# Banded attention and a gated product on one core: w_out decoded in pairs, more small buffers, and a new written order

## The chip, the core and the metric

The kernel runs on one core of a Trainium2 chip: TensorE for matrix products (PE in the profile, PEld its weight loads), VectorE (DVE), ScalarE (ACT), GpSimd (POOL) and SyncE (SP), which issues most DMAs; ScalarE issues the rest. All inputs lie in HBM, the result goes back there. The metric is the time of one execution on the device, in microseconds (us).

## The reference, cut to what matters

```python
# attention: batch 8, heads 8, 512 local and 32 global positions, head size 64
k_all, v_all = concat(k_g, k_l), concat(v_g, v_l)
out_g = sm(scale * q_g @ k_all.T) @ v_all            # global queries see all keys
s_ll = where(abs(i - j) <= 32, scale * q_l @ k_l.T, -1e9)
out_l = sm(concat(scale * q_l @ k_g.T, s_ll)) @ concat(v_g, v_l)
x = heads_joined(concat(out_g, out_l))               # [8, 544, 512]
# gated product
gate = sigmoid(sum(conv_w[k] * x shifted by k - 4 for k in range(5)))
out = (gate * (x @ w_val)) @ w_out                   # [8, 544, 512]
```

The weights w_val, conv_w and w_out arrive as 64-bit floats (their type in the reference is kept as it comes), and the kernel decodes them from pairs of 32-bit words on the chip.

## The kernel before, in words

A *unit* u (32 of them) is one batch with one pair of heads; batch b has units 4b to 4b+3. For each unit: `s` (score products into two PSUM banks, 64 small matmuls), `mx` (VectorE: mask, negated scale and row maximum, L490; for five early units the mask is added by TensorE and L486 takes the maximum), `exp` (ScalarE, L503), `den` and `rec` (VectorE), `norm` (scaling by the reciprocal, one half of a unit at a time, on VectorE L521 or as four ScalarE instructions L519), `t` (VectorE transposes, L528). Two units together give one product with the values, `av`. `xc` copies its result from PSUM, `halo` sets the four columns ahead of it, `xh` and `xl` split it into two parts that TensorE multiplies at its faster rate, `tap` and `conv` are the five taps of the convolution on VectorE (for four units TensorE does them with diagonal weights: `dg`, `pc`), and `sig` is the sigmoid.

The global queries go by batch: `gs` (scores), `gmax` and `gng` (maximum, negated), `gexp`, `gt` (transposes on TensorE), `gtc` (copy), `gav`, `gden`, `grec`, `gnorm`, `gx`, `gxc`.

The gated product goes by batch too: `g1.b.e.t` (three matmuls of 512 columns, L628, in which block t of x meets block e of w_val), `gv` (times the gate), `gh`, `gl` (the two parts again), `g2.b.r.e` (three matmuls, L665), `ob` (copy out of PSUM), `st` (store). A last, smaller pass with the key g does the global rows of all batches.

**The order** is a text, `ORDER`: a list of some 2,000 task names, which the program runs through once. Each engine gets its instructions in this order and keeps to it. A name's `:ACT`, `:DVE` or `:SP` says which engine does a task that several could do; `@36` says which of the eight PSUM banks it takes (`gs0@36`: banks 3, 4 and 6, 7). A task that writes a bank waits for all that still reads it. `z17.1` is 17 matmuls of zeros into bank 1: they fill TensorE's time at the start. A planner made the list; it is not in the program.

Loads go out on SP's queue in the list's order, and each one also waits until TensorE has done the last matmul that stands ahead of it in the list (`transfer`). A load whose buffer is still read holds up all that is behind it in the queue.

The weights are decoded in eight steps `s0` to `s7` (`f64_parts`) and a rounding `high`. The four column blocks of w_val are decoded in two pairs, with buffers that later hold gh and gl. The four row blocks of w_out are decoded singly, and take their raw words from a buffer of the attention's `pm` rotation and the working copy from the output's `ob` rotation.

Of the kernel before, what the change touches and what calls it, by code (L numbers as in the profile page):

```python
# [82 lines left out]
cw dg0:DVE s0@30 dg1:DVE dg2:ACT mx0.0 mx0.1 ng0 s1@52 dg3:DVE exp0.0 mx1.0 mx1.1 z6.0@1 gs0@36 exp0.1 ng1 s2@01  # L83
exp1.0 den0 rec0 norm0.1:DVE norm0.0:DVE t0 exp1.1 den1 w0.s0:ACT gmax0.0 rec1 norm1.0:ACT mx2.0 norm1.1:ACT gmax0.1
mx2.1 gng0 gexp0.0 w0.s1 ng2 exp2.0 exp2.1 t1 z17.1@5 av0@42 w0.s2 w0.s3 w0.s4 wi4 w0.high:ACT den2 w0.s5 w2.s0:ACT
gexp0.1 rec2 w0.s6 w2.s1 iq4 iq5 xc0:ACT z8.2@0 s3@07 w0.s7 norm2.1:ACT gt0.0@4 w2.s2 mx3.0 halo0 gt0.1@5 mx3.1
norm2.0:ACT t2 pc0.0@1 ng3 w4.s0:ACT ig3 xh0:ACT gtc0.0 gtc0.1 xc1:ACT w4.s1 ig2 w2.s3 exp3.0 exp3.1 w4.s2 xl0
w2.high:ACT w4.s3 pc0.1 pc0.2 wi5 pc0.3 w2.s4 w4.high:ACT ig0 ig1 s4@23 w4.s4 halo1 den3 iq6 iq7 w4.s5 rec3
norm3.0:ACT w4.s6 s5@05 pc0.4 norm3.1:DVE w5.s0:ACT mx4.0 mx4.1 xh1:ACT conv0.3:ACT pc1.0@7 w4.s7 ng4 w5.s1 pc1.1
pc1.2 exp4.0 t3 w5.s2 gav0@6 gden0 ig6 mx5.0 exp4.1 exp5.0 mx5.1 exp5.1 grec0 pc1.3 pc1.4 w5.s3 av1@20 w2.s5 gnorm0  # L90
gx0@6 den4 w5.s4 xc3:ACT gxc0:ACT xl1 conv1.3:ACT w5.high:DVE g1.0.1.0@5 ig5 xc2:ACT rec4 den5 w2.s6 w5.s5 iv2
halo2:DVE g1.0.1.1 gs1@60 halo3:DVE iq8 w5.s6 rec5 w5.s7 w2.s7 s6@23 mx6.0 gmax1.0 mx6.1 norm4.1:ACT gmax1.1
norm4.0:ACT xh2:DVE norm5.1:ACT pc2.0@4 pc2.1 exp6.0 gng1 pc2.2 pc2.3 iq9 ig4 fix0 exp6.1 pc2.4 pc3.0@3 den6 gexp1.0
xl2 gexp1.1 t4 pc3.1 gt1.0@6 gt1.1@0 ig7 xh3:DVE norm5.0:ACT pc3.2 conv2.3:ACT gtc1.0 iv3 fix1 s7@47 gtc1.1 rec6
norm6.0:ACT t5 mx7.0 wi6 s8@10 iq10 mx7.1 norm6.1:ACT g1.0.3.0@6 g1.0.0.0@4 t6 xl3 exp7.1 exp7.0 pc3.3 mx8.0 mx8.1
pc3.4 gav1@7 exp8.0 conv3.3:ACT w6.s0:DVE gden1 den7 w6.s1 g1.0.1.2 grec1 rec7 exp8.1 g1.0.0.1 sig0 w6.s2 norm7.1:DVE
# [89 lines left out]
FIRST = "q0 q1 w0 q2 q3 w1 v0 w2 w3 v1 m0"  # L186
NX = 10
XC = 3
NH = 9
NHF = 2  # L190
NV = 2
NPC = sum(f"pc{u}.0" in BY for u in range(NU))
# [6 lines left out]
def attention_moe(ctx, tc, qk, vw, vgw, maskd, fard, w_val, convT, w_out, out):  # L199
# [103 lines left out]
    def weight(k):  # L303
# [31 lines left out]
        for m in range(8):  # L335
            tasks[f"w{k}.s{m}"] = lambda m=m: step(m)
# [530 lines left out]
```

## Time and profile before

| | us |
|---|---|
| median of three runs | 344.08 (343.84 to 345.83) |
| the profiled execution | 342.64 |
| its span from first to last instruction | 340.9 |
| TensorE, busy in the span | 330.6 (97%) |
| VectorE | 319.5 (94%) |
| ScalarE | 285.0 (84%) |
| mean DMA rate | 178 GB/s, 60.67 MB in all |

The span is what the profile's times count from; the execution's own time is 1.7 us longer. Busy time is the union of an engine's instructions. Waits, branches and DMA issues are not in it. Ends of matmuls are modelled, so TensorE can be slower than its best pace and still show as busy.

### The profile page before, as it was taken

The numbers are of one execution on the slowest core, as the hardware profiler recorded it, in microseconds if no ns is written. First come the engines' busy times: TensorE is split into PE (matmuls) and PEld (weight loads), VectorE is DVE, ScalarE is ACT, GpSimd is POOL, SyncE is SP. The second block draws the span as 40 slices with busy tenths as digits, with TensorE's granted clock in tenths as the row PEclk, the third lists the DMA queues.
The fourth block names the chain that finished last, engine by engine and source line by source line (L and its number), as shares of the span: only waits on it lengthen the run. The fifth ranks groups of instructions, "written<-read, shape, count | busy, mean of one in ns | idle before, by whom it ended". The sixth has DMA issues, their size and how long they took to land.

```text
span 340.9 us, 15502 instructions
## 1 busy us (share of the span) xinstructions
PE 330.6 (97%) x6575; PEld 254.8 (75%) x6575; DVE 319.5 (94%) x987; ACT 285.0 (84%) x926; POOL 0.8 (0%) x7
## 2 busy tenths in 40 slices
PE   7899999999999999999999999999999999999995
PEld 4475566768877867788778687788787787888894
DVE  6899999999999999999899999999999998998981
ACT  3899999989999999999999899999998869314240
POOL 0000000000000000000000000000000000000000
PEclk9999999999999999999999999999999999999999
DMA  7969868726672358577845471596322712002032
GB/s 276 385 206 322 313 210 257 280 68 237 240 236 80 105 173 336 162 232 262 294 105 184 167 271 45 198 336 181 135 72 74 253 15 95 4 31 92 2 123 63
DMA packets 20037, 60.67 MB, mean 178 GB/s; under 512 B 2304, under 2 KB 4736, under 8 KB 19968
## 3 DMA queue, kind: packets, MB, share of 16 engines
q1 hardware_dynamic: 18528, 57.01, 48.8%
q10 hardware_dynamic: 1440, 2.67, 2.2%
q8 instruction: 51, 0.84, 1.0%
q14 instruction: 18, 0.15, 0.1%
HBM read 50.76 MB, written 8.91 MB: 175 GB/s over the span
## 4 chain that ended last, share of the span: by engine, by line
PE 83%; DMA 6%; ACT 5%; DVE 3%; issue 1%; ACTq 0%; SPq 0%; DVEq 0%
PE psum L628 28%; PE psum L665 25%; PE psum L542 10%; PE psum L469 8%; PE psum L606 4%; PE psum L422 3%; DMA wraw<-in_w_val_dram 3%; PE psum L404 2%; PE psum L381 2%; DMA vg<-in_vgw_dram 2%; ACT pm L519 1%; DMA qk<-in_qk_dram 1%; ACT pm L503 1%; ACT xc L284 1%; PE psum L439 1%
## 5 line engine op out<-in xcount | busy, mean ns | idle before, releaser
L503 ACT ACTIVATE pm<-pm,mx 128x128 f32<-128x128 f32 x216 | 83.9, 395 | 0.8 <-DVE mx L490 0.7
L588 DVE SCALAR_TENSOR_TENSOR gate<-xc,cw,gate 128x512 f32<-128x512 f32 x112 | 80.6, 744 | 0.8 <-ACT gate L278 0.3
L665 PE MATMUL psum<-woh,gh 128*128 128x512 f32 x128 | 52.2, 408 | 0.7 <-ACT pg L396 0.5
L628 PE MATMUL psum<-xh,wvh 128*128 128x512 f32 x128 | 52.7, 412 | 0.0
L628 PE MATMUL psum<-xh,wvl 128*128 128x512 f32 x128 | 50.6, 395 | 0.0
L628 PE MATMUL psum<-xl,wvh 128*128 128x512 f32 x128 | 50.5, 395 | 0.0
L519 ACT ACTIVATE pm<-pm,mx 128x128 f32<-128x128 f32 x160 | 50.5, 400 | 0.0
L665 PE MATMUL psum<-woh,gl 128*128 128x512 f32 x128 | 50.1, 391 | 0.0
L665 PE MATMUL psum<-wol,gh 128*128 128x512 f32 x128 | 50.1, 391 | 0.0
L490 DVE CUSTOM_DVE_ANT_0 pm<-psum,mask 128x128 f32<-128x128 f32 x216 | 48.4, 286 | 1.4 <-PE psum L469 1.3
L542 PEld LDWEIGHTS psum<-pts,v 32*64 32x64 f32 x2560 | 35.9, 130 | 8.2 <-issue 2.5
L503 ACT ACTIVATION_READ_ACCUMULATOR pm<-pm,mx 128x1 f32 x216 | 41.8, 194 | 0.0
L528 DVE STREAM_TRANSPOSE pts<-pm 128x1024 f32<-128x1024 f32 x32 | 39.4, 1235 | 0.5 <-ACT pm L519 0.3
L542 PE MATMUL psum<-pts,v 32*64 32x96 f32 (+3 forms) x2560 | 38.9, 259 | 0.8 <-ACT pg L396 0.6
L469 PE MATMUL psum<-qk 64*32 64x128 f32 x2048 | 36.3, 272 | 0.9 <-issue 0.5
L469 PEld LDWEIGHTS psum<-qk 64*32 64x32 f32 x2048 | 29.5, 105 | 7.5 <-issue 4.2
L665 PEld LDWEIGHTS psum<-woh,gh 128*128 128x128 f32 x128 | 24.1, 188 | 7.8 <-issue 1.4
L284 ACT COPY ob<-psum 128x512 f32<-128x512 f32 x30 | 17.4, 579 | 14.8 <-PE psum L665 13.6
L628 PEld LDWEIGHTS psum<-xh,wvh 128*128 128x128 f32 x128 | 24.3, 190 | 7.2 <-issue 1.0
L628 PEld LDWEIGHTS psum<-xh,wvl 128*128 128x128 f32 x128 | 24.0, 188 | 5.7
L665 PEld LDWEIGHTS psum<-woh,gl 128*128 128x128 f32 x128 | 24.0, 188 | 5.4
L628 PEld LDWEIGHTS psum<-xl,wvh 128*128 128x128 f32 x128 | 24.1, 188 | 4.6
(120 smaller groups left out, 542.1 us busy)
## 6 DMA issues: line engine op xcount, KB each, us to landing
qk<-in_qk_dram SPq DMA_DIRECT2D x30, 768.0 KB, 6.0
vg<-in_vgw_dram SPq DMA_DIRECT2D x32, 325.0 KB, 3.7
v<-in_vw_dram SPq DMA_DIRECT2D x16, 640.0 KB, 5.5
out_dram<-ob SPq DMA_DIRECT2D x26, 256.0 KB, 3.9
wraw<-in_w_val_dram SPq DMA_DIRECT2D x4, 512.0 KB, 11.1
wraw<-in_w_out_dram SPq DMA_DIRECT2D x4, 512.0 KB, 4.0
out_dram<-ob ACTq DMA_DIRECT2D x6, 256.0 KB, 2.0
qk<-in_qk_dram ACTq DMA_DIRECT2D x1, 480.0 KB, 3.8
```

The source lines that it names most:

```text
L284: A.copy(out, in_)
L422: on_pe(T.matmul(ag[SG * c:SG * c + SG, :], pgt[:, R * h + a if a < R else 2 * R, SG * c:SG * c + SG], vt[:, a, h, :], start=(a == 0), sto ...
L469: on_pe(T.matmul(s[h][C * j:C * j + C, i, :], qkt[rows, C * QAT[m]:C * QAT[m] + C], blocks(qkt[rows], b, (C * ahead, 2), (C * near, 2), (1 ...
L490: V.tensor_tensor_reduce(out=pm[:, h, i, :], in0=s[:, i, :], in1=mask[:, (c0 + i > 0) + (c0 + i == HB - 1), :], op0=ALU.add, op1=ALU.min, ...
L503: A.activation(out=pm[:, h, i, :], in_=st[u]["s"][h][:, i, :] if ON_PE[u] else pm[:, h, i, :], func=AF.Exp, bias=mx[:, c:c + 1], scale=SCA ...
L519: A.activation(out=p[:, i, :], in_=p[:, i, :], func=AF.Copy, scale=rec[:, i:i + 1])
L528: V.transpose(out=st[w, "pts"][:, :, R * k:R * k + R].rearrange("p h i a q -> p h (i a q)"), in_=st[u]["pm"].rearrange("p h i c -> p h (i ...
L542: on_pe(T.matmul(x[j // 2][D * h:D * h + D, j % 2, C * first:C * (first + count)], vt[rows, slot, h, :], p, start=(slot == 0), stop=stop))
L588: V.scalar_tensor_tensor(out=acc, in0=xc[:, k:k + SL], scalar=cw[:, u % NDT, k:k + 1], in1=acc, op0=ALU.mult, op1=ALU.add)
L606: on_pe(T.matmul(bank(f"pc{u}.0"), diag[n][:, c, :], st[u]["xc"][:, k:k + SL], start=(k == 0), stop=(k == KW - 1)))
L628: on_pe(T.matmul(bank(f"g1.{key}.{e}.0")[:, :n], w[:, e, t * P:t * P + P], x, start=(t == 0 and q == 0), stop=(t == NDT - 1 and q == 2)))
L665: on_pe(T.matmul(bank(f"g2.{key}.{r}.0"), g, w, start=(e == 0 and q == 0), stop=(e == NDT - 1 and q == 2)))
```

## The change

Three things change in the code, and the whole list of the order.

w_out is decoded in pairs like w_val: 1024 columns at a time, in 2 x 8 steps instead of 4 x 8. Its raw words get a buffer of their own (`wr`, one, for two pairs one after the other), the working copy too (`wa`). The statistics `mx` have six buffers instead of three, and each could hold two units; since the list still names `den` for every unit, every unit gets its own and den and rec stay as they were. Two buffer counts (`NPM`, `NPT`) keep their values under a name. The DMA scratch of the compiler is set to 1024.

The list is another one throughout. By its tags, on the whole: three halves of norm go from VectorE to ScalarE (40 to 43 on ScalarE), three xh casts (21 to 24), two ob copies (30 to 32) and the one gxc copy; four gh casts go from ScalarE to VectorE (11 to 15 there) and three xc copies (0 to 3). taps and halos keep their numbers, 14 loads of ScalarE's function tables stay 14. The zero matmuls at the start are 6, 12 and 13 instead of 6, 17 and 8.

```diff
 ORDER = """
-cw dg0:DVE s0@30 dg1:DVE dg2:ACT mx0.0 mx0.1 ng0 s1@52 dg3:DVE exp0.0 mx1.0 mx1.1 z6.0@1 gs0@36 exp0.1 ng1 s2@01
...
+cw dg0:DVE dg1:DVE s0@46 mx0.0 mx0.1 ng0 s1@10 dg2:DVE exp0.0 exp0.1 mx1.0 mx1.1 ng1 den0 exp1.0 rec0 norm0.0:DVE
...
@@ -187,6 +186,9 @@
 NX = 10
 XC = 3
 NH = 9
+NMX = 6
+NPM = 3
+NPT = 2
 NHF = 2
 NV = 2
 NPC = sum(f"pc{u}.0" in BY for u in range(NU))
@@ -267,7 +269,7 @@
 
     def taps():
         raw = craw.rearrange("p (n two) -> p n two", two=2)
-        a = rotating([P, NDT * KW], I32, tag="mx", name="cva", bufs=3)
+        a = rotating([P, NDT * KW], I32, tag="mx", name="cva", bufs=NMX)
         for step in f64_parts(raw, a, None):
             step()
         V.tensor_tensor(out=cw.rearrange("p t k -> p (t k)"), in0=a.bitcast(F32), in1=raw[..., 0].bitcast(F32),
@@ -303,19 +305,15 @@
     def weight(k):
         of_val = k < NDT
         c = k % NDT
-        n = 2 if of_val else 1
         src = w_val if of_val else w_out
         whi, wlo = (wvh, wvl) if of_val else (woh, wol)
         box = {}
 
         def load():
-            if of_val:
-                if c % 2 == 0:
-                    wraws["pair", c] = rotating([P, 2, 2 * DM], I32, tag=("gh", "gl")[c // 2], name=f"wraw{k}", bufs=1)
-                raw = wraws["pair", c // 2 * 2][:, c % 2]
-            else:
-                raw = box["raw"] = rotating([P, 1, 2 * DM], I32, tag="pm", name=f"wraw{k}", bufs=3)
-                raw = raw[:, 0]
+            if k % 2 == 0:
+                wraws["pair", k] = rotating([P, 2, 2 * DM], I32, tag=("gh", "gl")[c // 2] if of_val else "wr",
+                                           name=f"wraw{k}", bufs=1)
+            raw = wraws["pair", k // 2 * 2][:, k % 2]
             if of_val:
                 transfer(raw.rearrange("p (t n) -> p t n", t=NDT),
                          src[:, c * P:c * P + P].bitcast(I32).rearrange("(t p) n -> p t n", p=P))
@@ -324,17 +322,18 @@
 
         def step(m):
             if m == 0:
-                raw = wraws["pair", c] if of_val else box["raw"]
-                raw = raw.rearrange("p w (n two) -> p w n two", two=2)
-                box["a"] = rotating([P, n, DM], I32, tag="pts" if of_val else "ob", name=f"wa{k}", bufs=2)
-                box["steps"] = f64_parts(raw, box["a"], wlo[:, c:c + n, :], lambda m: BY[f"w{k}.s{m}"])
+                raw = wraws["pair", k].rearrange("p w (n two) -> p w n two", two=2)
+                tag, bufs = ("pts", NPT) if of_val else ("wa", 1)
+                box["a"] = rotating([P, 2, DM], I32, tag=tag, name=f"wa{k}", bufs=bufs)
+                box["steps"] = f64_parts(raw, box["a"], wlo[:, c:c + 2, :], lambda m: BY[f"w{k}.s{m}"])
             box["steps"][m]()
 
         wraws[k] = load
         tasks[f"wi{k}"] = load
-        for m in range(8):
-            tasks[f"w{k}.s{m}"] = lambda m=m: step(m)
-        tasks[f"w{k}.high"] = lambda: copy(f"w{k}.high", whi[:, c:c + n, :], box["a"].bitcast(F32))
+        if k % 2 == 0:
+            for m in range(8):
+                tasks[f"w{k}.s{m}"] = lambda m=m: step(m)
+            tasks[f"w{k}.high"] = lambda: copy(f"w{k}.high", whi[:, c:c + 2, :], box["a"].bitcast(F32))
 
     loads, values = {}, {}
 
@@ -472,13 +471,17 @@
         st[u] = {"s": s}
 
     def open_p(u):
-        st[u]["pm"] = rotating([P, 2, R, P], F32, tag="pm", name=f"pm{u}", bufs=3)
+        st[u]["pm"] = rotating([P, 2, R, P], F32, tag="pm", name=f"pm{u}", bufs=NPM)
 
     def l_max(u, h):
         s = st[u]["s"][h]
         c0 = R * (u % 2)
         if h == 0:
-            st[u]["mx"] = rotating([P, 16], F32, tag="mx", name=f"mx{u}", bufs=3)
+            if u % 2 == 0 or f"den{u}" in BY:
+                both = rotating([P, 2, 16], F32, tag="mx", name=f"mx{u}", bufs=NMX)
+            else:
+                both = st[u - 1]["both"]
+            st[u]["both"], st[u]["mx"] = both, both[:, u % 2 if f"den{u // 2 * 2 + 1}" not in BY else 0]
             if not ON_PE[u]:
                 open_p(u)
         pm, mx = st[u].get("pm"), st[u]["mx"]
@@ -504,12 +507,15 @@
                          bias=mx[:, c:c + 1], scale=SCALE if ON_PE[u] else -1.0,
                          accum_out=mx[:, 8 + c:9 + c])
 
+    def sums(u):
+        return st[u]["mx"][:, 8:16] if f"den{u // 2 * 2 + 1}" in BY else st[u]["both"][:, :, 8:16]
+
     def l_den(u):
-        den = st[u]["mx"][:, 8:16]
+        den = sums(u)
         V.tensor_scalar(out=den, in0=den, scalar1=1e-9, scalar2=None, op0=ALU.add)
 
     def l_rec(u):
-        den = st[u]["mx"][:, 8:16]
+        den = sums(u)
         V.reciprocal(den, den)
 
     def l_norm(u, h):
@@ -523,7 +529,7 @@
     def l_turn(u, h):
         w, k = divmod(u, 2)
         if (w, "pts") not in st:
-            st[w, "pts"] = rotating([P, 2, HB, R, C], F32, tag="pts", name=f"pts{w}")
+            st[w, "pts"] = rotating([P, 2, HB, R, C], F32, tag="pts", name=f"pts{w}", bufs=NPT)
         if h is None:
             V.transpose(out=st[w, "pts"][:, :, R * k:R * k + R].rearrange("p h i a q -> p h (i a q)"),
                         in_=st[u]["pm"].rearrange("p h i c -> p h (i c)"))
@@ -850,7 +856,7 @@
     from concourse.bass_utils import run_bass_kernel_spmd as _run
 
     laid = _layout(_np, **inputs)
-    nc = _bacc.Bacc("TRN2", target_bir_lowering=False, num_devices=1)
+    nc = _bacc.Bacc("TRN2", target_bir_lowering=False, num_devices=1, dynamic_dma_scratch_size=1024)
     arrays, args = {}, []
     for name in _INS:
         a = _np.ascontiguousarray(laid[name])
```

Three places in the instruction order follow. Names there are tiles: gm is the maximum of the global scores, mx and pm the statistics and exponentials of a unit, wraw a weight's raw words, wa its working copy.

VectorE in batch 2, where the global scores' maximum is taken. Before:

```order
L259 SCALAR_TENSOR_TENSOR wol<-wraw_1090 128x512
L389 TENSOR_REDUCE gm_1413<-psum 128x1 x2
L490 ISA pm_1421,mx_1420<-psum,mask 128x128
L490 ISA mx_1420 128x1
L490 ISA pm_1421,mx_1420<-psum,mask 128x128
L490 ISA mx_1420 128x1
L490 ISA pm_1421,mx_1420<-psum,mask 128x128
L490 ISA mx_1420 128x1
L490 ISA pm_1421,mx_1420<-psum,mask 128x128
L490 ISA mx_1420 128x1
L393 TENSOR_SCALAR gm_1413<-gm_1413 128x2
L642 TENSOR_TENSOR gl_1334<-gv_0_1335,gh_1333 128x512
```

and now:

```order
L260 TENSOR_SCALAR wraw_1006<-wa_1127 128x1024
L288 CAST gh_1303<-gv_0_1305 128x512
L642 TENSOR_TENSOR gv_1_1371<-psum,gate_952 128x512
L388 TENSOR_REDUCE gm_1374<-psum 128x1
L288 CAST gh_1303<-gv_1_1371 128x512
L388 TENSOR_REDUCE gm_1374<-psum 128x1
L648 TENSOR_TENSOR gl_1304<-gv_1_1371,gh_1303 128x512
L392 TENSOR_SCALAR gm_1374<-gm_1374 128x2
L493 ISA pm_1400,mx_1399<-psum,mask 128x128
L493 ISA mx_1399 128x1
```

Before, the negation (L393) stands behind four mask steps and their reads of the accumulator; now (L392) it stands ahead of all of them, and the two maxima have other work between them.

ScalarE near the start, from the first decode step of the second w_val pair to the copies of the transposed global block (pgt). Before:

```order
L248 ACTIVATE wa_477<-wraw_99 128x1024
L396 ACTIVATE pg<-psum,gm_343 128x544
L284 COPY xc_487<-psum 128x512
L519 ACTIVATE pm_362<-pm_362,mx_350 128x128 x8
L248 ACTIVATE wa_568<-wraw_472 128x512
L284 CAST xh_572<-xc_487 128x512
L410 COPY pgt_575<-psum 128x512
L410 COPY pgt_575<-psum 128x640
L284 COPY xc_578<-psum 128x512
L503 ACTIVATE pm_584,mx_551<-psum,mx_551 128x128 x8
```

and now:

```order
L250 ACTIVATE wa_499<-wraw_99 128x1024
L286 COPY xc_506<-psum 128x512
L286 CAST xh_555<-xc_506 128x512
L409 COPY pgt_563<-psum 128x512
L280 ACTIVATE diag_235<-ident,cw 128x128
L280 ACTIVATE diag_570<-ident,cw 128x128 x4
L525 ACTIVATE pm_476<-pm_476,mx_370 128x128 x4
L409 COPY pgt_563<-psum 128x640
L286 CAST wvh<-wa_499 128x1024
L506 ACTIVATE pm_587,mx_576<-psum,mx_576 128x128 x8
L506 ACTIVATE pm_675,mx_674<-pm_675,mx_674 128x128 x4
```

The second pgt copy (128x640) stood right behind the first; now five diagonal pieces and a scaling of four stand between the two, and the second xc copy with its xh cast ahead of both.

SyncE's queue around the last loads of w_out. Before:

```order
L296 DMA v_1039<-in_vw_dram 128x1280
L296 DMA wraw_1090<-in_w_out_dram 128x1024
L296 DMA qk_1124<-in_qk_dram 128x1536
L296 DMA qk_1230<-in_qk_dram 128x1536
L296 DMA vg_1237<-in_vgw_dram 128x650
L296 DMA wraw_1342<-in_w_out_dram 128x1024
L296 DMA vg_1533<-in_vgw_dram 128x650
```

and now:

```order
L298 DMA vg_974<-in_vgw_dram 128x650
L298 DMA wraw_1006<-in_w_out_dram 128x1024 x2
L298 DMA v_1084<-in_vw_dram 128x1280
L298 DMA qk_1099<-in_qk_dram 128x1536
L298 DMA qk_1180<-in_qk_dram 128x1536
L298 DMA v_1294<-in_vw_dram 128x1280
```

Before, the four blocks of w_out were loaded at four places of the queue; now there are two, two loads each, and the second, which needs the buffer of the first, has the v load of the third pair of units right behind it.

## Rows read from the trace of the kernel before

**Rows 1.** busy time of each engine over the span, from the page.

```profile
PE 330.6 (97%) x6575; PEld 254.8 (75%) x6575; DVE 319.5 (94%) x987; ACT 285.0 (84%) x926; POOL 0.8 (0%) x7
```

**Rows 2.** stages: us, then busy PE, PEld, DVE, ACT, POOL, granted clock, DMA.

```profile
30.00:165.00 135.00, 133.67 (x3096) 99.33 (x3096) 132.36 (x478) 132.76 (x456) 0.00 (x0) 1.00 0.63 217
165.00:205.00 40.00, 39.02 (x794) 30.66 (x793) 38.04 (x132) 37.29 (x121) 0.00 (x0) 1.00 0.58 193
205.00:290.00 85.00, 84.68 (x1851) 67.38 (x1850) 82.58 (x236) 76.98 (x240) 0.00 (x0) 1.00 0.43 141
290.00:335.00 45.00, 45.00 (x298) 38.01 (x281) 39.88 (x80) 14.02 (x30) 0.00 (x0) 1.00 0.13 48
```

**Rows 3.** timeline at 205 us: start, duration, engine, line, operation, tiles.

```profile
205.37 0.40 PE L628 MATMUL psum<-xh,wvh 128*128 128x512 f32 x1
205.04 0.29 DVE L490 CUSTOM_DVE_ANT_0 pm<-psum,mask 128x128 f32<-128x128 f32 x1
205.25 0.29 DVE L490 CUSTOM_DVE_ANT_0 pm<-psum,mask 128x128 f32<-128x128 f32 x1
205.47 0.69 DVE L584 TENSOR_TENSOR xl<-xc,xh 128x512 fp32r<-128x512 f32 x1
```

**Rows 4.** groups by shape: operation, tiles, count, busy us, mean ns, idle before.

```profile
L256 DVE SCALAR_TENSOR_TENSOR wa<-wraw,wa 128x512 int32<-128x512 int32 x4 | 2.7, 678 | 0.0
L256 DVE SCALAR_TENSOR_TENSOR wa<-wraw,wa 128x1024 int32<-128x1024 int32 x2 | 2.4, 1217 | 0.0
L263 DVE TENSOR_SCALAR wraw<-wraw 128x512 int32<-128x512 int32 x4 | 1.7, 429 | 0.0
L263 DVE TENSOR_SCALAR wraw<-wraw 128x1024 int32<-128x1024 int32 x2 | 1.4, 725 | 0.0
L286 DVE CAST gh<-gv 128x512 fp32r<-128x512 f32 x10 | 4.2, 422 | 0.0
L280 DVE TENSOR_SCALAR gate<-xc,cw 128x512 f32<-128x512 f32 x7 | 3.3, 467 | 0.0
L286 DVE CAST xh<-xc 128x512 fp32r<-128x512 f32 x11 | 4.6, 417 | 0.2 <-ACT xc L284 0.2
L286 DVE COPY xc<-xgT 128x4 f32<-128x4 f32 x15 | 2.2, 162 | 0.0
L503 ACT ACTIVATE pm<-pm,mx 128x128 f32<-128x128 f32 x216 | 83.9, 395 | 0.8 <-DVE mx L490 0.7
L284 ACT CAST gh<-gv 128x512 fp32r<-128x512 f32 x22 | 13.4, 616 | 8.5 <-DVE gv L636 8.5
L278 ACT ACTIVATE gate<-xc,cw 128x512 f32<-128x512 f32 x21 | 15.3, 728 | 0.0
L284 ACT CAST xh<-xc 128x512 fp32r<-128x512 f32 x21 | 13.2, 628 | 0.2
L519 ACT ACTIVATE pm<-pm,mx 128x128 f32<-128x128 f32 x160 | 50.5, 400 | 0.0
L615 ACT ACT_TABLE_LOAD x7 | 9.0, 1283 | 0.1
```

**Rows 5.** waits: who for whom, us in total, times, longest.

```profile
PEld psum L665 <- ACT pg L396: 1.4, 2, 0.9
PEld psum L542 <- ACT pg L396: 1.3, 2, 1.0
```

**Rows 6.** timeline of the table load in batch 5 and of who waits.

```profile
192.31 1.28 ACT L396 ACT_TABLE_LOAD   x1 [1.64 <-DVE gm L393]
194.37 0.19 PEld L665 LDWEIGHTS psum<-woh,gh 128*128 128x128 f32 x1 [0.94 <-ACT pg L396]
```

**Rows 7.** stages again, for the granted clock behind the busy times.

```profile
12.00:14.00 2.00, 0.50 (x15) 0.23 (x19) 1.85 (x5) 2.00 (x14) 0.00 (x0) 1.00 1.07 373
339.00:340.00 1.00, 0.00 (x0) 0.00 (x0) 0.00 (x0) 0.00 (x0) 0.00 (x0) 0.73 0.54 163
```

**Rows 8.** loads of w_out: queue, count, KB each, median us from issue to landing.

```profile
wraw<-in_w_out_dram SPq DMA_DIRECT2D x4, 512.0 KB, 4.0
```

## What I expect of the change

> **What bounds the kernel now.** I read the page's busy line first, then the stage table, then single moments on two engines. The busy line [rows 1] shows three engines nearly full at once: TensorE 97%, VectorE 94%, ScalarE 84%. The stage table [rows 2] says who is full where. From 30 to 165 us VectorE is busy 132.36 of 135, ScalarE 132.76 and TensorE 133.67. From 165 to 205 it is 38.04, 37.29 and 39.02 of 40. From 205 to 290 TensorE has 84.68 of 85, VectorE 82.58, ScalarE only 76.98. From 290 to 335 TensorE is busy all 45.00, VectorE 39.88, ScalarE 14.02. So up to about 205 us all three hold each other, and after that it is TensorE alone. A busy TensorE is not one at its peak (ends of matmuls are modelled), so the engine to count on up to 205 us is VectorE, whose busy time is real.
>
> The moment I count from is the score product of the global queries of batch 6 (gs6). In the changed order it stands behind exactly the TensorE tasks that, before, stood ahead of the first group of batch 4, g1.4.0.0: I compared the two lists, they differ only in the start-up zero matmuls, and there the sum is 6+17+8 = 31 before and 6+12+13 = 31 after. Before, TensorE reaches that point at 205.37 us [rows 3].
>
> **The change part by part.**
>
> *VectorE up to that point.* gs6 takes a PSUM bank in which the scores of unit 25 lie, so it waits for that unit's second mask step, mx25.1, on VectorE. Before, VectorE finishes mx24.1 just before it starts the next instruction at 205.47 [rows 3]. How much work stands in VectorE's list ahead of those two points?
> - The decoding of w_out: four times seven instructions of 512 columns become two times seven of 1024. Three of the seven are of the L256 kind, 678 ns against 1217, four of the L263 kind, 429 against 725 [rows 4]. By means: 4 x (3 x 0.678 + 4 x 0.429) = 15.0 us, now 2 x (3 x 1.217 + 4 x 0.725) = 13.1 us: 1.9 less. But means overlap: the two L490 rows start 0.21 us apart and last 0.29 each [rows 3], so an instruction that goes saves about 0.08 less than its mean. Fourteen fewer take 1.1 of the 1.9 back: 0.8 to 1.9 less.
> - Three gh casts more (0.422 each), three taps more (0.467), two xh casts fewer (0.417) [rows 4]: 1.27 + 1.40 - 0.83 = 1.8 more. One w_out high part fewer (the nearest row is the same kind of cast, 0.42) and three 4-column halo copies fewer (0.162 each [rows 4]): 0.9 less, 0.6 with the overlap. One magnitude step is twice as wide: 0.3 more, by the L263 rows. The number of scalings is the same, eight have changed places.
> - Sum: between 0.7 less (-1.9 +1.8 -0.9 +0.3) and 0.7 more (-0.8 +1.8 -0.6 +0.3). I take nothing, the middle: **the new order asks of VectorE, ahead of the same TensorE work, what the old one did.** All that can be won up to 205 us is idle time of VectorE: 135 - 132.36 = 2.6 us, and 40 - 38.04 = 2.0 us [rows 2], 4.6 in all.
>
> *ScalarE up to that point.* Here the list does get shorter: two half units of exp fewer (8 x 0.395 = 3.2 us), three gh casts fewer (3 x 0.616 = 1.8), three taps fewer (3 x 0.728 = 2.2), two xh casts more (2 x 0.628 = 1.3) [rows 4]; the rest (fewer but wider decode steps, one copy and five halo copies more) brings some 1 back. That is about 5 less. ScalarE was as full as VectorE there, so part of VectorE's idle time was waiting for it. This is the reason to expect some of the 4.6 back. I take a third, 1.5 us: nothing says more, since a chain through three full engines always leaves some gaps, and nothing says less than none.
>
> *The wait for the exp table.* At 192.31 ScalarE loads the exp table only when the maximum of the global scores is there, and TensorE, whose next group writes a bank of these scores, stands until 194.37, 0.94 us idle before it [rows 6]. In all, weights waited 1.4 us for that activation, in two places [rows 5]. In the new order gs5 has other banks, and five groups of three matmuls and a score product stand between it and the first matmul that needs the exponential. In batch 2 the maximum is negated ahead of the mask steps instead of behind four of them. A load's row is 1283 ns, with 0.1 us idle ahead of seven of them [rows 4]; so I expect the stand of 0.94 to shrink. Most of it lies inside VectorE's idle time too; 0.3 I count by itself. The Trainium skill ("ScalarE: Activation LUTs", section "What ACT_TABLE_LOAD costs") gives a switch about 2.66 us, of which 1.38 are a drain. The rows show the load and no drain. By the page the exponential would come 1.4 us later and that 0.3 would not be won.
>
> *Buffers.* w_out gets one raw buffer for two pairs and a buffer of its own for the decode, instead of the attention's pm and the output's ob buffers. The loads of the first pair then wait for nothing. The second pair waits for the last step of the first on VectorE, and behind it in SP's queue stand a v load and two qk loads; the first user of that v is av2, ahead of which VectorE still has two units' mask steps, two transposes and half a decode, and w_out loads land 4.0 us after issue [rows 8]. So I cost this at nothing. Six statistic buffers instead of three take waits away and cost nothing. The small DMA scratch only makes room: the kernel has no DMA from GpSimd.
>
> *After gs6.* What VectorE no longer has to do there is 3 scalings and more, but TensorE is the bound: its idle 0.3 us (85 - 84.68) is all that I count. What ScalarE did not do before, it does here: 5 us plus what is moved to it for good (three scalings of 4 x 0.400 [rows 4], three xh casts and two output copies more, four gh casts and three xc copies fewer: about 2), so 77.0 becomes some 84 of the 85 us between 205 and 290. If this stays off TensorE's path it costs nothing; if not it is the third rival.
>
> *Sum.* -1.5 (idle of VectorE) -0.3 (table) -0.3 (late idle) = -2.1 us. The profiled execution took 342.64 us (span 340.9), which makes 340.5; it lies 1.4 under the median of the runs, 344.08. The forecast is for the median: 344.1 - 2.1 = **342.0 us**, 0.6% less.
>
> **Rivals.**
> 1. *Most of the idle time goes.* If VectorE is kept full, 4.6 + 0.6 = 5.2 us are won: 338.9; two thirds of it give 340.6. For it: ScalarE's shorter list. Against: VectorE was already 98% busy. Chance 0.20, range 338.9 to 340.6.
> 2. *The change does not do what it says.* A new order with the same work ahead of the same points has as many gaps as the old one, in other places. 343.3 to 345.5, middle 344.1. For it: VectorE's equal sums. Chance 0.15.
> 3. *ScalarE becomes the bound after 205 us (slower).* It gets 7 us more between 205 and 290, where it had 8 idle. If those 8 are waits that can't be filled (its idle time there was mostly waiting for matmuls and products), exp and output copies come late, banks stay taken and TensorE waits. It decides from the point where more than 1 us of ScalarE's idle time stays; if all does, 7 us are lost: 344.1 - 2.1 + 7 = 349.0. Against: the exponentials are done well ahead there, ScalarE is nearly free after 290. Chance 0.13, 344 to 349.
> 4. *TensorE's clock falls at the start (slower).* In the new order score product s4 needs a bank of the transposed global block, whose copy ScalarE reaches only behind a diagonal of five pieces and a scaling of four. ScalarE has 15 instructions there (0.4 us and more each [rows 4]), TensorE after av0 only three small pieces and s3, so I estimate a pause of 2 to 3 us near 30 us. A pause of 1.5 us between 12 and 14 us left the granted clock at 1.00; at the end, over two us after the last matmul, it had fallen (0.73 in the stretch) [rows 7]. The pause lies between the two. Matmuls at 1.2 instead of 2.4 GHz take twice as long; TensorE's work between 31 and 40 us can't be more than these 9 us, so 9 us is the bound: 342.0 + 9 = 351. The Trainium skill ("TensorE: Matmul & The Clock Gate", "What's actually happening") says that idleness brings the 1.2 GHz back; that the trace shows at the end alone. Chance 0.05.
>
> **Numbers.** The forecast, 340.6 to 343.3, has 0.47. The range takes in rival 1 but for its lowest end, rival 2, and the lower part of rivals 3 and 4: 339.2 to 346.0. About 1% (3.4 us) is what a measurement can tell here. Faster by more than that means under 340.6: rival 1 and a little of the forecast, 0.23. Slower means over 347.5: two thirds of rivals 3 and 4 (0.18 together), whose prices reach from little to 7 and 9 us, 0.12. Within 1%: 0.65.
>
> **What would show it.** Right: gs6 (the L380 group of batch 6) starts between 202 and 206 us; VectorE's idle time from 30 us to there falls from 4.6 to about 3; TensorE's wait for the exponential of batch 5 is under 0.4 us; ScalarE between gs6 and 290 is over 95% busy without TensorE waiting on it. The forecast is wrong if gs6 comes before 201 us (my sums of VectorE are off, or its idle time was cheap to remove), or if TensorE shows several us of waits behind ScalarE after it (rival 3), or a granted clock under 1.00 near 30 us (rival 4).

## The result and the profile after

| kernel | median us (lowest to highest) | runs |
|---|---|---|
| before | 344.44 (342.56 to 350.69) | 13 |
| after | 340.70 (339.46 to 343.87) | 13 |

The ratio is 0.990, 95% interval 0.9867 to 0.9933: 3.4 us less, by the interval 2.3 to 4.6: just the 1% that the prediction called the limit of what can be told. (The ratio leaves out executions that fell in a slow state of the chip, so it is not the quotient of the two medians.) The forecast was 342.0, with 339.2 to 346.0 as its range. The two profiled executions lie 3.2 us apart (342.64 and 339.46), and they are compared here.

The mean granted clock does not explain the gain. Seven of the 13 runs after had 0.998 or more, 26 of the 90 runs of the kernel before that went with the experiments. Their medians are 339.9 and 343.7; those of the other runs are 341.8 and 344.6. So it is 2.8 to 3.8 us at like clock.

First the page of the kernel after, busy time of each engine in the order of [rows 1]. VectorE has 2.3 us less and ScalarE 2.1 more.

```profile
PE 328.3 (97%) x6575; PEld 254.4 (75%) x6575; DVE 317.2 (94%) x970; ACT 287.1 (85%) x934; POOL 0.8 (0%) x7
```

The stage table of after, with the columns of [rows 2]. VectorE's idle time from 30 to 205 us was 2.64 + 1.96 = 4.6, and is 1.10 + 0.63 = 1.7. TensorE, which had 0.98 idle between 165 and 205, has none there, and none up to 290; of its 1.81 between 30 and 165, one pause near 30 us is 1.76. ScalarE between 205 and 290 has 77.99, not the 84 of the forecast.

```profile
30.00:165.00 135.00, 133.19 (x3081) 100.11 (x3083) 133.90 (x453) 133.86 (x462) 0.00 (x0) 1.00 0.66 217
165.00:205.00 40.00, 40.00 (x942) 31.52 (x925) 39.37 (x152) 39.28 (x131) 0.00 (x0) 1.00 0.63 205
205.00:290.00 85.00, 85.00 (x1816) 68.35 (x1805) 82.71 (x232) 77.99 (x244) 0.00 (x0) 1.00 0.41 137
```

Fixed times mix what is done earlier with what is done faster, so the same view is cut where the work is the same. First the kernel before, up to the point that answers to gs6 (205.37 us [rows 3]) and 84.63 us on; then the kernel after, with gs6 at 202.79. Columns as above.

```profile
0.00:205.37 205.37, 199.40 (x4439) 148.02 (x4440) 196.36 (x675) 194.00 (x658) 0.85 (x7) 1.00 0.65 224
205.37:290.00 84.63, 84.31 (x1849) 67.08 (x1848) 82.21 (x232) 76.61 (x238) 0.00 (x0) 1.00 0.43 141
```

```profile
0.00:202.79 202.79, 196.96 (x4438) 147.22 (x4439) 196.32 (x663) 191.45 (x652) 0.85 (x7) 1.00 0.67 225
202.79:287.42 84.63, 84.63 (x1882) 67.94 (x1882) 82.47 (x230) 78.38 (x248) 0.00 (x0) 1.00 0.43 144
287.42:337.70 50.28, 46.69 (x278) 39.28 (x261) 38.42 (x79) 17.30 (x35) 0.00 (x0) 0.99 0.16 58
```

The reader is to see two things. VectorE's work up to gs6 is the same to 0.04 us (196.36 and 196.32), and the 2.58 us that gs6 comes earlier are its idle time (9.01 and 6.47). ScalarE has 2.55 us less. From gs6 to the end the gain is only 135.53 - 134.91 = 0.6.

The waits for the global exponential [rows 5], 1.4 and 1.3 us of weight loads before, are one short row in the whole list of waits after. (PEld is the weight load ahead of a matmul; the matmuls' own waits were shorter, 0.5 and 0.6 us.)

```profile
PEld psum L548 <- ACT pg L395: 0.4, 1, 0.4
```

The timeline of after, batch 5 (start, duration, engine, line, operation; [rows 6] of before). ScalarE has other work up to 188.40, loads the table, and ends the exponential at 190.50. TensorE starts g2.3.3.0 at 188.78, in a bank that has nothing to do with it, and never stands. The last row is the first matmul of gs6.

```profile
188.21 0.19 ACT L286 COPY xc<-xgT 128x4 f32<-128x4 f32 x1
188.50 1.28 ACT L395 ACT_TABLE_LOAD   x1
188.78 0.40 PE L671 MATMUL psum<-woh,gh 128*128 128x512 f32 x1
189.79 0.71 ACT L395 ACTIVATE pg<-psum,gm 128x544 f32<-128x544 f32 x1
...
202.79 0.63 PE L380 MATMUL psum<-qk 64*32 64x480 f32 x8
```

### The profile page after: what moved, and what is told of

It is laid out like the page before. It is cut to its first block, busy times and chain, and to the rows that moved or that the text cites. A ratio compares the mean times of both kernels' runs of the same rounds, so it can differ in the third digit from the quotient of the medians.

```text
span 337.7 us, 15486 instructions
## 1 busy us (share of the span) xinstructions
PE 328.3 (97%) x6575; PEld 254.4 (75%) x6575; DVE 317.2 (94%) x970; ACT 287.1 (85%) x934; POOL 0.8 (0%) x7
## 4 chain that ended last, share of the span: by engine, by line
PE 85%; ACT 9%; DMA 4%; issue 0%; ACTq 0%
PE psum L634 26%; PE psum L671 26%; PE psum L548 10%; PE psum L468 8%; PE psum L612 5%; DMA qk<-in_qk_dram 4%; PE psum L421 3%; PE psum L380 2%; ACT pm L525 2%; PE psum L403 2%; PE psum L717 2%; ACT pm L506 1%; PE psum L660 1%; ACT xh L286 1%; ACT xc L286 1%; ACT pgt L409 1%
## 5 line engine op out<-in xcount | busy, mean ns | idle before, releaser
L506 ACT ACTIVATE pm<-pm,mx 128x128 f32<-128x128 f32 x216 | 84.2, 403 | 0.1
L525 ACT ACTIVATE pm<-pm,mx 128x128 f32<-128x128 f32 x172 | 54.4, 403 | 0.0
L506 ACT ACTIVATION_READ_ACCUMULATOR pm<-pm,mx 128x1 f32 x216 | 43.5, 201 | 0.0
L468 PE MATMUL psum<-qk 64*32 64x128 f32 x2048 | 35.5, 272 | 0.0
L621 ACT ACTIVATE gate<-gate 128x512 f32<-128x512 f32 x32 | 19.5, 632 | 9.3 <-DVE gate L594 8.8
```

The lines of the kernel that those rows point to most:

```text
L468: on_pe(T.matmul(s[h][C * j:C * j + C, i, :], qkt[rows, C * QAT[m]:C * QAT[m] + C], blocks(qkt[rows], b, (C * ahead, 2), (C * near, 2), (1 ...
L506: A.activation(out=pm[:, h, i, :], in_=st[u]["s"][h][:, i, :] if ON_PE[u] else pm[:, h, i, :], func=AF.Exp, bias=mx[:, c:c + 1], scale=SCA ...
L525: A.activation(out=p[:, i, :], in_=p[:, i, :], func=AF.Copy, scale=rec[:, i:i + 1])
L621: A.activation(out=g, in_=g, func=AF.Sigmoid)
```

## The experiments

Three theories stood against each other: the gain is the *waits for the global exponential* that are gone (batches 2 and 5); it is the *decoding in pairs*, with less work for VectorE; it is the *fit of the whole list*, many small gaps. The buffers of w_out and the DMA scratch got no run of their own. All ratios are to the kernel before, whose median was 344.4 to 344.5 in all sets.

| run | median us | ratio, 95% interval |
|---|---|---|
| E1 old list, then new | 343.66 | 0.9976 (0.9954 to 0.9999) |
| E2 new list, then old | 345.78 | 1.0049 (1.0013 to 1.0084) |
| E3 old, the two waits shortened | 343.59 | 0.9960 (0.9928 to 0.9992) |
| E4 old, pairs only | 348.61 | 1.0107 (1.0074 to 1.0139) |
| E5 new, one wait put back | 342.64 | 0.9961 (0.9929 to 0.9992) |
| E6 new, decoded singly | 342.35 | 0.9946 (0.9919 to 0.9973) |
| E7 new, three statistic buffers | 341.52 | 0.9922 (0.9893 to 0.9951) |
| E8 new, 14 zero matmuls more | 351.38 | 1.0199 (1.0165 to 1.0232) |
| E9 new, the 31 zeros redivided | 340.76 | 0.9898 (0.9863 to 0.9933) |
| E10 new, six casts and taps on ScalarE | 343.88 | 0.9986 (0.9954 to 1.0017) |
| E11 new, both waits put back | 344.10 | 0.9998 (0.9967 to 1.0029) |
| E12 E9 with halos on GpSimd | 340.53 | 0.9894 (0.9859 to 0.9929) |

**E1 and E2: the two lists joined.** At 123 us both lists have given TensorE the same tasks.

```diff
 cw dg0 ... (E1: the old list, E2: the new list, up to the point)
-the rest of this list
+the other list's tasks that are not done yet, in its order
```

> The old list up to its task g1.2.1.0 (123.54 us in the old trace; the new trace reaches the same TensorE work 0.68 us sooner), from there the new list; code, decoding and buffers are the old ones. Theory 'two waits for the global exponential' (batch 2 at 73 us, batch 5 at 192 us): only the second is gone, about -1.5 to -2.0 us against before. Theory 'decode in pairs frees VectorE': the old decode stands, 0. Theory 'the new list simply has smaller gaps everywhere': -2.1, what the new trace wins after that point.

> The new list, decode and buffers up to the same point (122.86 us in the new trace), from there the old list. Two waits: batch 2's is gone, batch 5's stays: -0.5 to -1.0 us against before. Decode in pairs: all of the gain is there, -2.5 to -3. Smaller gaps everywhere: -0.7, what the new trace has won at that point.

E1 gave -0.8 us, E2 +1.7. No theory had both. The parts don't add up to the whole (-3.4), because each seam brings its own waits, as the traces show. The waits of E1 after the seam: an output copy waits for a store that is late, and TensorE 0.9 us for the copy.

```profile
ACT ob L284 <- DMA out_dram<-ob: 1.9, 1, 1.9
```

In E2, with the old list's batch 5, TensorE waits for the exponential again, longer than in the kernel before (0.5 there for the same row):

```profile
PE psum L671 <- ACT pg L395: 1.7, 2, 1.2
```

So this pair does not settle where the gain lies. It shows that a list is fitted to what ran ahead of it.

**E3: the waits shortened in the old kernel.**

```diff
-mx9.0 gng2
+gng2 mx9.0
-gexp5.0 norm21.0:DVE t20 gh.3.3:ACT gl.3.3 mx23.0 xh19:ACT mx23.1 g2.3.2.2 g2.3.3.0@2
+gh.3.3:ACT gl.3.3 xh19:ACT gexp5.0 norm21.0:DVE t20 mx23.0 mx23.1 g2.3.2.2 g2.3.2.3 g2.3.1.2 g2.3.1.3 g2.3.3.0@2
```

> The old kernel with two small moves: in batch 2 the negation gng2 stands ahead of the mask step mx9.0; in batch 5 ScalarE does a gh and an xh cast ahead of the global exponential instead of behind it, and TensorE does three groups that don't need a bank of the global scores ahead of g2.3.3.0. Two waits: most of the gain comes back, -1.5 to -2.8 us. Decode in pairs, and smaller gaps everywhere: -0.5 to +0.3.

-1.4 us by the ratio, interval -0.3 to -2.5: the two waits alone, in the old list, give some two fifths of the gain. The forecast for this theory was 1.5 to 2.8, so this is just under its lower edge. The trace of before has nearly the same price. The matmul behind each wait, and the one ahead of it:

```profile
75.07 0.39 PE L665 MATMUL psum<-woh,gl 128*128 128x512 f32 x1
76.02 1.21 PE L542 MATMUL psum<-pts,v 32*64 32x256 f32 x57 [0.56 <-ACT pg L396]
...
193.48 0.39 PE L665 MATMUL psum<-woh,gl 128*128 128x512 f32 x1
194.37 0.50 PE L665 MATMUL psum<-woh,gh 128*128 128x512 f32 x1 [0.50 <-ACT pg L396]
```

In batch 5 the starts are 0.89 us apart, where these matmuls otherwise start 0.23 apart, and the next start is 0.1 late too: 0.76 lost. In batch 2 they are 0.95 apart, where the new kernel has 0.33 at such a change of operation: 0.62. That is 1.4 us together. (The profiled execution of E3 took 348.7, five over the median; why, the last section says.)

**E4: the pairs alone in the old list.**

```diff
-w4.s0 ... w4.s7, w5.s0 ... w5.s7 (512 columns each)
+w4.s0 ... w4.s7 (1024 columns), at about every second one of these places
```

> The old list with w_out decoded in pairs from buffers of its own (each pair's step at about the place of the old second steps; loads in pairs), statistic buffers three as before. Decode in pairs: VectorE has 0.8 to 1.9 us less to do, and -0.8 to -1.9 us comes out. Two waits, and smaller gaps everywhere: between -0.4 and +0.4.

3.7 us slower, where the theory of the decoding wanted 0.8 to 1.9 faster. One wait of its trace:

```profile
90.42 0.50 PE L671 MATMUL psum<-wol,gh 128*128 128x512 f32 x1 [1.70 <-DVE wol L261]
```

A pair is ready only when both halves are, and the old list uses the third block of w_out too early for that. Part of the cost is thus my placing of the steps. So E4 does not price the pairs: it shows that, put into the old list at these places, they bring no gain.

**E5 and E11: the waits put back into the new kernel.** E5 exchanges two banks; every engine keeps its instructions in their order. E11 also moves one small negation.

```diff
-g2.3.3.0@2 ... gexp5.0 gt5.0@6
+gexp5.0 g2.3.3.0@6 ... gt5.0@2
-gng2 mx9.0                       (E11 only)
+mx9.0 gng2
```

> The new kernel with two banks exchanged in batch 5: g2.3.3.0 takes bank 6, where the scores gs5 lie, and gt5.0 takes bank 2. Every engine keeps its instructions and their order; TensorE now has to wait for the global exponential there (in the new trace it ends at 190.50 us, g2.3.3.0 starts at 188.78: 1.7 us). If waits for the global exponential are what the new list took away: 1.0 to 1.7 us more than the new kernel, 341.7 to 342.4. If VectorE alone sets the pace there and hides it: 0 to 0.5 more.

> The new kernel with both waits for the global exponential put back: in batch 5 the two banks exchanged (alone 342.6 us), and in batch 2 the negation gng2 behind the mask step mx9.0 as in the old list (0.93 us later; in the new trace the product av3 starts 0.4 us after the exponential's end). If these waits are the gain: 343.3 to 344.0, three quarters or more of the way back to 344.5. If VectorE hides the one of batch 2: 342.6.

E5 took 342.64, 1.9 over the new kernel's median (the theory of the waits said 1.0 to 1.7). Its timeline: the bank comes free when the exponential ends (190.28 + 0.71), and TensorE stands 1.63 us for it, though it has other work in its list.

```profile
189.03 0.39 PE L634 MATMUL psum<-xh,wvl 128*128 128x512 f32 x1
190.28 0.71 ACT L395 ACTIVATE pg<-psum,gm 128x544 f32<-128x544 f32 x1
...
191.05 0.50 PE L671 MATMUL psum<-woh,gh 128*128 128x512 f32 x1 [1.63 <-ACT pg L395]
```

From 189.03 to 191.05 the starts are 2.02 apart instead of 0.23, and the next start is 0.1 late: 1.9 lost, the 1.9 of the median. So this is not the old wait of batch 5 but one two and a half times as dear.

E11 took 344.10, ratio 0.9998: **two exchanged banks and one moved negation undo the whole gain.** The same two places in its timeline:

```profile
77.29 0.98 PE L548 MATMUL psum<-pts,v 32*64 32x256 f32 x36 [0.16 <-ACT pg L395]
...
191.93 0.50 PE L671 MATMUL psum<-woh,gh 128*128 128x512 f32 x1 [1.62 <-ACT pg L395]
```

They are not the old sizes either: TensorE's idle time is 0.16 us in batch 2 (0.56 before) and 1.62 in batch 5 (0.50 before). And the clock has a part in the 1.5 us between E5 and E11: eight of E5's 12 runs had a mean of 0.998 or more, three of E11's. So E11 does not show that the old waits were the whole gain.

**E6 and E7: the other parts of the change taken out.**

```diff
-box["steps"] = f64_parts(raw, box["a"], wlo[:, c:c + 2, :], on)
+one, two = (f64_parts(raw[:, h:h + 1], ...) for h in range(2))        # E6, w_out only
+box["steps"] = [lambda x=x, y=y: (x(), y()) for x, y in zip(one, two)]
-NMX = 6
+NMX = 3                                                               # E7
```

> The new kernel with each step of the decoding of w_out issued as two instructions of 512 columns at the same place instead of one of 1024 (15 instructions more on VectorE, one on ScalarE); buffers, loads and list as in the new kernel. If VectorE's work is what counts between 30 and 85 us: 0.8 to 1.9 us more than the new kernel's 340.7. If the gain comes from waits alone and VectorE has slack: 0 to 0.4 more.

> The new kernel with three statistic buffers instead of six. Prediction's step on buffers (they cost and bring nothing): within 0.3 us of the new kernel's 340.7. If the wider rotation is what let VectorE run ahead: VectorE waits for scalings and transposes of a unit three back, 1 us or more added.

E6 is 1.6 us over the new kernel's median and 0.8 over E7's from the same set; the intervals overlap both. The theory of the decoding wanted 0.8 to 1.9. E6's trace, of the fastest of its nine runs (340.97), reaches gs6 179.9 us after the first product av0, the new kernel 179.8. So 15 more instructions of VectorE show as 0.1 us there; what decoding in pairs is worth stays open. E7, 0.8 over, is not to be told from the new kernel.

**E8 and E9: zero matmuls at the start.**

```diff
-z6.0@2 ... z12.1@7 ... z13.2@7
+z20.0@2 ... z12.1@7 ... z13.2@7        (E8: 45 in all)
+z16.0@2 ... z8.1@7 ... z7.2@7          (E9: 31 as before)
```

> The new kernel with 20 instead of 6 zero matmuls ahead of the first global scores, so that TensorE has work up to about 13.7 us, where it paused from 11.7 to 14.2 for a load. In four of four experiments' profiles the granted clock read 0.50 to 0.74 in the two us after that pause, and runs of the new kernel with a mean clock of 0.995 are 1 to 2 us above those with 0.998 to 1.000. If the pause brings the slow stretch: mean clock 0.998 or more in every run and a median of 339.5 to 340.2. If it comes by itself: no change, 340.7, or 0.5 more where the zeros hold up the scores.

> The new kernel with its 31 zero matmuls divided as 16, 8 and 7 instead of 6, 12 and 13: the early pause is bridged, and every later TensorE instruction keeps its number in the program. With 14 zeros added (45) the time was 351.4 us, and its trace has six stands of 1.4 to 2.1 us, all a whole multiple of about 255 TensorE instructions apart. If those stands come from where the program is cut into blocks for fetching: none of them here, 339.3 to 340.7, and a mean clock of 0.998 or more where the bridge works. If the early zeros themselves hold up the program: 343 or more.

E8 missed by 10 us; its trace is in the last section. E9 stands with the new kernel (340.76). The early pause and the granted clock behind it (the third number from the end of a row), first in E7, then in E9:

```profile
12.00:14.00 2.00, 0.23 (x6) 0.14 (x11) 1.53 (x4) 2.00 (x14) 0.00 (x0) 1.00 1.09 380
16.00:18.00 2.00, 2.00 (x6) 1.51 (x6) 2.00 (x7) 1.49 (x4) 0.00 (x0) 0.50 1.13 363
```

```profile
12.00:14.00 2.00, 1.62 (x19) 0.41 (x23) 1.90 (x5) 2.00 (x13) 0.00 (x0) 1.00 1.10 386
16.00:18.00 2.00, 1.53 (x48) 1.09 (x48) 1.97 (x7) 1.71 (x5) 0.00 (x0) 1.00 1.13 361
```

With most of the pause filled (TensorE busy 1.62 of these two us instead of 0.23), all six runs of E9 have a mean clock of 0.998 or more and lie within 339.7 to 341.7; of the new kernel's 13 runs six had 0.990 or 0.995, and those took 340.7 to 343.9. The spread is smaller, the median not: at 0.998 or more E9's 340.8 is 0.9 over the new kernel's 339.9. Its start is longer (TensorE does the same work 1.1 us later by 80 us, 80.35 and 79.22 in the two traces).

**E10: work back to ScalarE.**

```diff
-gh.2.0:DVE gh.2.1:DVE gh.2.2:DVE tap8:DVE tap10:DVE tap11:DVE
+gh.2.0:ACT gh.2.1:ACT gh.2.2:ACT tap8:ACT tap10:ACT tap11:ACT
```

> The new kernel with three gh casts (2.0 to 2.2) and three taps (8, 10, 11) on ScalarE again, where the old list had them: about 2.4 us less for VectorE, 3.6 more for ScalarE between 110 and 160 us. Prediction's step on ScalarE (its shorter list is what gives VectorE's idle time back): slower by 1 us or more. VectorE as the engine to count on: faster by 1 to 2.4 us. Waits for the global exponential as the whole story: within 0.5 us of the new kernel's 340.7.

3.2 us slower than the new kernel: as the step on ScalarE wanted. VectorE has less to do (118.36 us instead of 120.25 in the stretch shown under E12) and waits for ScalarE; the waits between 123 and 160 us:

```profile
DVE gl L648 <- ACT gh L286: 1.8, 1, 1.8
...
DVE gate L594 <- ACT gate L280: 1.0, 1, 1.0
DVE gate L594 <- ACT xc L286: 1.0, 1, 1.0
```

This counts against the waits for the exponential as the whole story: it is another wait that takes back nearly as much.

**E12: a third engine.**

```diff
-halo2:DVE halo3:DVE halo4:DVE ... halo31:DVE (15 on VectorE, 15 on ScalarE)
+halo2:POOL halo3:POOL halo4:POOL ... halo31:POOL
```

> The new kernel with its zero matmuls divided 16, 8, 7 and its 30 four-column halo copies on GpSimd, which has nothing to do after the start. Up to gs6 there are nine of them each on VectorE and ScalarE, of 0.161 and 0.196 us: 1.4 and 1.8 us less work for the two full engines. If work on these two is all that is left to win up to 205 us: 339.3 to 340.0 (0.8 to 1.5 less than the 340.8 of the divided zeros). If a copy on GpSimd comes later than the first convolution step needs it, or holds VectorE up: 341 or more, with VectorE waiting on xc from GpSimd.

340.53: no gain beside E9's 340.76, though a copy takes GpSimd only 0.34 us (mean of 30; the median is 0.19, the longest 1.23) and nobody waits for it. Why, the stage rows show. They go from one point to another between which TensorE has the same 2,688 matmuls in every list (from g1.0.3.3's place before, gt2.0's after, to g2.3.0.1): the kernel before, after, E12, E10 and E11, in this order; E6 takes 121.36 and E9 121.59.

```profile
79.15:203.23 124.08, 122.88 (x2688) 96.47 (x2686) 121.06 (x421) 121.00 (x399) 0.00 (x0) 1.00 0.62 210
```

```profile
79.22:200.65 121.43, 121.38 (x2687) 96.59 (x2686) 120.25 (x430) 120.04 (x399) 0.00 (x0) 1.00 0.59 193
```

```profile
79.64:200.98 121.34, 121.25 (x2688) 96.37 (x2686) 119.83 (x424) 119.35 (x390) 4.67 (x13) 1.00 0.60 192
```

```profile
79.00:202.88 123.88, 122.25 (x2688) 96.53 (x2686) 118.36 (x424) 123.18 (x405) 0.00 (x0) 1.00 0.59 188
```

```profile
80.43:204.11 123.68, 121.55 (x2687) 96.29 (x2686) 120.60 (x430) 120.38 (x401) 0.00 (x0) 1.00 0.59 189
```

TensorE's busy time for these matmuls is 121.25 to 121.6 in five of the kernels, and wherever the new list runs undisturbed the stretch takes just that. Less work for VectorE and ScalarE (E12) no longer shortens it. The kernel before took 2.65 us more than after. The wait of batch 5 is 0.76 of that, and that of batch 2 lies ahead of the stretch: some 1.9 us are other gaps, which no run prices one by one. E10 takes 2.45 more, with ScalarE busy 123.18 of 123.88; E11 2.25 more, with TensorE idle 2.13.

## Why the prediction was right, and where it was mis-sized

The time, 340.70, lies in the range, and 0.1 us above the upper end of the first rival's (338.9 to 340.6). Of the three terms of the sum the one for the table was mis-sized, 0.3 for 1.4.

**VectorE's equal sums: right.** Nothing was taken, between -0.7 and +0.7; the two traces say -0.04. The point chosen (the same TensorE tasks) made this readable.

**The idle time that comes back: right in kind, too small.** A third of VectorE's 4.6 us, 1.5, plus 0.3 for the table were to bring gs6 1.8 us earlier; it came 2.58 earlier, and 2.9 of the 4.6 are gone, nearly the two thirds of the first rival. "Nothing says more" was the failing sentence. A row that said more stood in [rows 2]: TensorE was idle 1.33 and 0.98 us in the same two stages. If TensorE sets the pace once it runs without a stand, as the stretches under E12 say, VectorE's whole 4.6 can't be won: the first rival's 5.2 us were not to be had by this list. Part of the 4.6 was the echo of TensorE's stands, which is the next point.

**The wait for the table: the term that was mis-sized.** Forecast: the stand of 0.94 shrinks to under 0.4 (it is gone), and is worth 0.3 by itself because the rest lies inside VectorE's idle time. The 0.94 of [rows 6] is the weight load's idle time; the matmul's was 0.50, and TensorE lost 0.76 there. The wait of batch 2, which I had named and given no price, lost 0.62. Together they are 1.4 us of the 2.58, and E3, which takes away these two, has -1.4. By this count, which no run makes by itself, 1.2 are left for the rest of the list, against the forecast's 1.5. The stand of TensorE was not hidden in the idle time of VectorE; VectorE's idle time was partly its consequence. E5 shows it: the output copy behind the stand comes late on ScalarE, a scaling behind the copy too, and VectorE's transpose waits for the scaling. In the new kernel the copy waits 0.18 us and the transpose not at all.

```profile
197.16 0.59 ACT L286 COPY ob<-psum 128x512 f32<-128x512 f32 x1 [2.09 <-PE psum L671]
198.95 1.25 DVE L534 STREAM_TRANSPOSE pts<-pm 128x1024 f32<-128x1024 f32 x1 [1.39 <-ACT pm L525]
```

So do the stage rows from 122.86 us to the same point of the program, E5 first, then the new kernel. With nothing changed but the two banks, VectorE is idle 2.87 us (80.37 - 77.50) instead of 0.87. Of the 2.58 us between the two stretches, 0.48 arose ahead of the stand (the matmul before it starts at 189.03 and 188.55) and are not the edit's.

```profile
122.86:203.23 80.37, 78.64 (x1742) 62.28 (x1740) 77.50 (x272) 76.89 (x254) 0.00 (x0) 1.00 0.64 213
```

```profile
122.86:200.65 77.79, 77.79 (x1741) 62.16 (x1740) 76.92 (x272) 76.85 (x254) 0.00 (x0) 1.00 0.66 221
```

Still the waits are not the sum of the gain: E3 brings 1.4 us of it in the old list, and E10 loses 3.2 without an edit at them. What the new list has, and each of E5, E10 and E11 takes away, is a stretch from 79 to 201 us in which TensorE never stands (121.38 busy of 121.43).

On the table itself: in the new trace ScalarE's copy ends at 188.40 and the load starts at 188.50, lasts 1.28, and the exponential follows at 189.79. The 1.38 us of drain that the Trainium skill ("ScalarE: Activation LUTs", section "What ACT_TABLE_LOAD costs") gives a switch are not in these rows; an estimate with them has the exponential end at 191.9.

**ScalarE: the direction right, the size half.** Its list up to gs6 was to be about 5 us shorter; it is 2.55 shorter (194.00 to 191.45). That this matters is shown by E10. The other half of the statement was wrong: between gs6 and 290 ScalarE was to be 95% busy, and is 78.38 of 84.63 us. Less had been moved there than I counted, and of it 2.9 us lie behind that stage, where ScalarE is nearly free (17.30 of 50.28, 14.39 before). The "about 2" that was to be moved for good is 3.6 by the means of its own terms; the page shows 2.1 in all. So the third rival never came near its price.

**Buffers: as forecast. Decoding: open.** Three statistic buffers are not to be told from six (E7). The pairs bring nothing in the old list as placed there (E4); in the new one taking them out costs 1.6 us by the medians, 0.1 by the traces (E6).

**After gs6:** 0.3 forecast, 0.6 measured in one pair of executions; too little to tell.

**The clock rival: the wrong place.** The pause near 30 us is there, 1.76 us, and the granted clock stayed 1.00 (stage row of after, 30 to 32 us):

```profile
30.00:32.00 2.00, 0.24 (x11) 0.13 (x16) 2.00 (x4) 2.00 (x7) 0.00 (x0) 1.00 0.48 133
```

What does fall is the clock behind the pause near 12 us, which both lists have, in some executions and not in others: 0.50 in E7 above, 1.00 in [rows 7] and in the profiled execution after. It fell behind one stand of 2.21 us too, in E8 (last section).

## What to carry to other kernels

When several engines are nearly full, look for the stands of the one that none can work around (here TensorE), and price each by how far apart the starts lie, not by its idle time; the idle time of the others is partly its echo. Compare traces at points where one engine has the same tasks behind it: equal work and lost time then separate to some tenths of a us. A wait that is put back is to be measured too, before its cost is taken for that of the old one. And gains of a fitted order don't add: two exchanged bank numbers can take back more than half of them.

## What was not expected of the hardware

Fourteen zero matmuls more at the start (E8) cost 10.7 us, though the start itself is not later (the first product av0 starts at 23.25 us, 22.95 in the new kernel). Its timeline has six stands of TensorE for which no wait is shown ("issue"):

```profile
81.45 0.40 PE L671 MATMUL psum<-woh,gh 128*128 128x512 f32 x1 [2.21 <-issue]
...
100.36 0.27 PE L468 MATMUL psum<-qk 64*32 64x128 f32 x1 [1.37 <-issue]
...
124.64 0.31 PE L548 MATMUL psum<-pts,v 32*64 32x32 f32 x5 [1.40 <-issue]
...
178.75 0.31 PE L421 MATMUL psum<-vg,pgt 128*32 128x65 f32 x5 [1.51 <-issue]
...
291.67 0.39 PE L634 MATMUL psum<-xl,wvh 128*128 128x512 f32 x1 [1.55 <-issue]
...
300.70 0.24 PE L548 MATMUL psum<-pts,v 32*64 32x32 f32 x2 [1.35 <-issue]
```

Together 9.4 us of the 13.1 that lie between the profiled executions of E8 and of the new kernel. Behind the first, the longest, the granted clock fell, and this may have a part in the rest; behind the other five it stayed at 1.00.

```profile
83.00:85.00 2.00, 2.00 (x7) 1.61 (x6) 0.00 (x0) 0.12 (x1) 0.00 (x0) 0.50 0.35 72
```

How many matmuls and weight loads TensorE has issued by each stand, from the stage rows of E8 that end in it:

```profile
0.00:80.50 80.50, 74.03 (x1754) 50.59 (x1755) 74.57 (x225) 70.05 (x248) 0.85 (x7) 1.00 0.79 269
0.00:99.70 99.70, 91.58 (x2137) 64.41 (x2138) 89.97 (x293) 85.76 (x297) 0.85 (x7) 0.98 0.71 240
0.00:124.00 124.00, 114.46 (x2648) 82.73 (x2649) 112.72 (x374) 107.59 (x369) 0.85 (x7) 0.99 0.65 219
0.00:178.00 178.00, 167.06 (x3797) 124.23 (x3798) 164.82 (x542) 160.51 (x554) 0.85 (x7) 0.99 0.66 221
0.00:291.00 291.00, 278.19 (x6097) 212.58 (x6098) 273.46 (x882) 266.62 (x893) 0.85 (x7) 0.99 0.60 198
0.00:300.00 300.00, 285.87 (x6352) 218.97 (x6353) 280.22 (x894) 270.59 (x899) 0.85 (x7) 0.99 0.58 192
```

That is 3509, 4275, 5297, 7595, 12195 and 12705: steps of 766, 1022, 2298, 4600 and 510, which are 3, 4, 9, 18 and 2 times 255 to 256. The page lists the queue that brings instructions:

```profile
q8 instruction: 51, 0.84, 0.9%
```

The program's 13,178 matmuls and weight loads over 51 transfers are 258 each; for which engines the transfers are the page does not say. So the stands look like blocks of TensorE's program that came late. The zeros are not needed for it: the profiled execution of E3, whose list has 31 zeros as the kernel before, has such a stand, the longest of all, and the clock was 0.50 from 165 to 167 us behind it.

```profile
163.26 1.23 PE L542 MATMUL psum<-pts,v 32*64 32x96 f32 x70 [2.73 <-issue]
```

```profile
0.00:162.00 162.00, 153.75 (x3414) 111.96 (x3414) 152.91 (x516) 150.60 (x519) 0.85 (x7) 0.99 0.66 229
```

It stands behind 6,828 instructions of TensorE, 3,319 or 13 times 255.3 behind the first of E8. Shorter ones at this spacing are in other traces (0.48 us in the kernel before at 169 us, 0.68 in E11 at 38 us). E9, where the 31 zeros are only divided otherwise, has none over 0.3 us at this spacing: its one long "issue" stand, 1.66 us ahead of av0, is off this spacing and ends just behind VectorE's transpose (20.89 + 1.24). Shown are thus the spacing and what the stands cost. That the fetch is the cause is argued, and why a block is late in one execution or list and not in another is open. A trace is to be checked for "issue" stands before its time is believed, above all after an edit that adds or removes instructions on TensorE.
